# A decode attention kernel on one core: the last 64 rows of wq land as half rows on all 128 partitions, and the filler products of the tail are regrouped

## The chip, the core and the metric

The kernel runs on one core of one Trainium2 chip. The core has five engines that run side by side and meet at semaphores: TensorE (PE, matrix products and weight loads), VectorE (DVE), ScalarE (ACT), GpSimd (POOL) and SyncE (SP, which here only issues transfers). Sixteen DMA engines carry the transfers. The metric is the device time of one execution in microseconds; a change is judged by the median of several runs against runs of the kernel before on the same chip.

## The reference

Two independent problems, A and B, are computed and their outputs laid side by side. Each is one decode step (one query per sequence) of attention over a cache window with two query heads per cache head:

```
B, Sq, D = 2, 1, 576;  Hq, Hkv, Sk, Dh = 32, 16, 16384, 128
W = min(4096, max(256, Sk // 4))                      # 4096: the last 4096 cache rows
q = (x @ wq).reshape(B, Sq, Hq, Dh).transpose(0, 2, 1, 3)
k = repeat(k_cache[:, :, Sk - W:, :], 2, axis=1)      # v the same
p = softmax(einsum("bhqd,bhkd->bhqk", q, k) * Dh ** -0.5)
o = einsum("bhqk,bhkd->bhqd", p, v)
out = o.transpose(0, 2, 1, 3).reshape(B, Sq, Hq * Dh) @ wo
```

All tensors are bfloat16. wq is 576 x 4096 and wo is 4096 x 576 in each problem. The cache windows are what is large: 1 MB for each problem, batch and cache head, 128 MB in all for K and V.

## The kernel before

**Slabs and the ring.** Everything large goes through `ring`, four buffers of 128 partitions x 32 KB (4 MB each). The list `stream` (lines 198 to 206) gives the order: the first 512 rows of wq for A, the same for B, then K and V slabs alternating (K0, K1, V0, K2, V1, ...), each slab holding four (batch, head) pairs of 4096 cache rows. SP issues all of these transfers in that order (`issue_slab`, `issue_wq`, `issue_wo`); before it issues slab n it waits until the reader of slab n-4 is done, because that is the buffer it overwrites. The pieces of wo (`wob`) are issued at fixed places of the stream. The last V slab is cut in two pieces (`PIECES`: three quarters and one quarter of it). The wo rows of the last group come as one transfer for the heads of the group's first slab and three for those of its second slab: heads (0,1), head 2 and head 3 (`HEADS`, `issue_last`), each with its own semaphore.

**The front.** D is 576 = 4 x 128 + 64, so wq is four chunks of 128 rows (the ring slab) and 64 remaining rows. `issue_wq` lands these remaining rows in the tile `wqr`, which has 128 partitions: A's rows on the even partitions and B's on the odd ones, 8 KB a row. x of the two problems sits in `x_sb` on four partitions (two per problem). For the chunk of remaining rows, line 361 copies each of the 64 values to two neighbouring columns, multiplied by a mask (`maskP`) that keeps only the column of the own problem (`x_dup`); then `f_xT` (line 346) transposes the five chunks on PE, and `f_xev` (line 367, ACT) spreads them into the stationary operand `xT`, which has `NXC` = 5 chunks per problem. `do_qpair` (line 396) makes q for two groups of heads at a time: five chunks times four banks, 20 products of 128 x 512, in two operations of which the first ends with the last product of the first group. Even pairs write the score banks `st`, odd pairs the banks `tb0`, `tb1`, `ot` and `acc`; `do_qrow` (ACT, then DVE, then ACT) takes q out of a group's banks. The third pair uses the banks of the first again and waits for them, and so on (`prev`).

**The middle.** For each K slab, DVE transposes it in four pieces (line 485), PE makes the scores (line 510 and its repeats through the helper at line 170), DVE finds the maxima, ACT takes the exponentials, DVE transposes the result, and PE multiplies it with the V slab (line 601). Every two slabs the heads of a group are normalised, spread (`do_redist`) and multiplied with wo (`do_proj`). The order of all this is written out by hand in lines 804 to 893; each engine works its list in order, and an instruction waits on semaphores for what it depends on.

**The tail.** After the last K slab come, on PE: the product with the first piece of the last V slab; `do_redist` of the last group (line 882), with two filler products of 128 x 512 on data that nobody reads (`f_idle`, line 711); the product with the second piece; two more filler products with a weight load of their own (`keep_on`, line 727, called at line 884); the collection of the last slab's heads (line 648); the product of the last group's first four heads with wo (line 760, which also waits for the last of `fin_ops`, DVE's copy at line 783 of the sums so far into the bank of the outputs); and the products of the last four heads, of which heads (0,1), head 2 and head 3 each wait for their own piece of wo. Then ACT and DVE take half of B's outputs each (lines 792 and 793), and two transfers write them.

Of the kernel before, what the change touches and what calls it, by code (L numbers as in the profile page):

```python
# [59 lines left out]
def build_kernel(nc, probs, out, cfg=None):  # L60
    cfg = dict(cfg or {})
    NR = cfg.get("NR", 4)
# [6 lines left out]
    NPROB = len(probs)  # L69
    Bb, _one, D = x0.shape  # L70
    _, Hkv, Sk, Dh = k0.shape
    HD = wq0.shape[1]
# [14 lines left out]
    DREM = D - 128 * NFC  # L87
    assert DREM * 2 == 128 and NFC * HD == SLABW
    HH = HD // 2
    NXC = NFC + 1  # L90
    NOUT = wo0.shape[1]
    NH = NOUT // 2
    NB0 = 512
# [13 lines left out]
    with es:  # L107
        sb = lambda name, shape, dt: es.enter_context(nc.sbuf_tensor(name, shape, dt))
        ring = sb("ring", [128, NR, SLABW], BF16)
        xt = sb("xt", [128, NKT, 2048], FP32)  # L110
        wqr = sb("wqr", [128, HD], BF16)
        wob = sb("wob", [128, 2, 8, NOUT], BF16)
        xT = sb("xT", [128, NXC, NPROB, 128], BF16)
        x_dup = sb("x_dup", [NPROB * Bb, DREM, NPROB], BF16)
        maskP = sb("maskP", [NPROB * Bb, NPROB], BF16)
# [44 lines left out]
        ring_sem = [sem("ring%d" % r) for r in range(NR)]  # L160
        wq_sem = sem("wq")
        wo_sem = [sem("wo%d" % r) for r in range(2)]
        x_sem = [sem("xload%d" % P) for P in range(NPROB)]
        wl_sem = [sem("wl%d" % n_) for n_ in range(len(HEADS))]
        out_sem = sem("outdone")
        piece_sem = [sem("piece%d" % n_) for n_ in range(NPC)]
# [15 lines left out]
            return op  # L182

        def load_x(P, eng):
            return dma_op(eng, x_sem[P], 1, lambda e: e.dma_start(
                x_sb[P * Bb:(P + 1) * Bb, :], probs[P][0][:, 0, :]).then_inc(x_sem[P], 16), [], "xload%d" % P)
# [57 lines left out]
        def issue_wq(n, P):  # L244
            wqP = probs[P][3]
            r = n % NR
            deps = [reader[n - NR]] if n >= NR else []
            wq_dma[P] = dma_op("sp", wq_sem, 1, lambda e: e.dma_start(
                wqr[P::NPROB, :], wqP[NFC * 128:D, :]).then_inc(wq_sem, 16), [], "wqr%d" % P)
            slab_dma[n] = dma_op("sp", ring_sem[r], 1, lambda e: e.dma_start(  # L250
                ring[:, r, :], wqP[0:NFC * 128, :].rearrange("(p s) n -> p (s n)", s=NFC)).then_inc(ring_sem[r], 16), deps, "wq%d" % P)

            if P == 0:
                for P_ in range(1, NPROB):
                    x_dma[P_] = load_x(P_, "sp")
# [89 lines left out]

        def f_xT(e, bank):
            last = None
            bb = bank[:].bitcast(BF16)
            NB = NPROB * Bb
            for ch in range(NXC):  # L350
                if ch < NFC:
                    src = x_sb[0:NB, 0:NFC * 128].rearrange("b (p s) -> b s p", s=NFC)[:, ch, :]
                else:
                    src = x_dup[0:NB, :, :].rearrange("b r t -> b (r t)")
                last = e.transpose(bb[:, ch * NB:(ch + 1) * NB], src, ident_b[0:NB, 0:NB])  # L355
            return last
        issue_until(0)
        init_small()
        init["maskP"] = S.add("dve", lambda e: e.tensor_reduce(
            maskP[:], ident_b[0:NPROB * Bb, 0:NPROB * Bb].rearrange("d (p b) -> d p b", b=Bb), AX.X, ALU.max), [p_ident_b], "maskP")  # L360
        x_cd = S.add("dve", lambda e: e.tensor_tensor(  # L361
            x_dup[:], x_sb[:, NFC * 128:D].unsqueeze(2).broadcast_to([NPROB * Bb, DREM, NPROB]),
            maskP[:].unsqueeze(1).broadcast_to([NPROB * Bb, DREM, NPROB]), ALU.mult), [init["maskP"]] + list(x_dma.values()), "xdup")

        n_x, bank_x, op_xT = tb_job(f_xT, "xT", list(x_dma.values()) + [x_cd, p_ident_b])

        def f_xev(e):
            NB = NPROB * NXC
            return e.activation(
                xT[:].rearrange("c h p (a w) -> c (h p) a w", a=4)[:, :, :, 0:Bb],  # L370
                bank_x[:].bitcast(BF16)[:, 0:NB * Bb].rearrange("c (p b) -> c p b", b=Bb).unsqueeze(2).broadcast_to([128, NB, 4, Bb]),
                ACTF.Copy)
        op_xev = S.add("act", f_xev, [op_xT, p_zxT], "xev")
        tb_consumer[n_x] = op_xev

        def init_mask():
# [318 lines left out]
        def do_redist(G, idle=0):  # L695
# [14 lines left out]
            if idle:  # L710
                def f_idle(e):
# [11 lines left out]
            tb_consumer[n] = r_ev[G]  # L723

        fin_ops = []

        def keep_on(n):
            def f(e):
                first = last = e.matmul(idle_out, ident_b[:, :], maskB[:, :], start=True, stop=True)
# [264 lines left out]
```

## Time and profile before

| what | value |
|---|---|
| median of three runs | 363.33 us (363.29 to 363.35) |
| the profiled execution's own time | 363.62 us |
| its span, first to last instruction | 362.3 us |
| DMA: moved, mean rate | 153.27 MB, 423 GB/s |
| busy share of the span | PE 62%, DVE 56%, ACT 19%, POOL 10% |
| first wqr transfer: issue at, landing after | 0.80 us, 3.7 us |
| second wqr transfer: issue at, landing after | 2.41 us, 13.2 us |
| first q product | at 15.70 us |
| last PE product | 360.25 us and 0.31 us long |

The span is what the profile covers; the own time of the profiled execution is 1.3 us longer, for what lies around the program. Busy shares are averages over the whole span and matmul ends are modelled. A row of a group list gives the line, the engine, the operation, output and input tile, the number of instructions, the busy time and the mean of one, and the idle time before them with what ended it. A row of a timeline gives start, length, and what. Names such as `st` stand for both buffers `st0` and `st1`.

### The profile page before, as it was taken

How to read it: one execution, taken by the hardware profiler on the slowest of the kernel's cores; microseconds unless marked ns; L12 is line 12 of the kernel's file. 1: busy time of each engine (PE TensorE's matmuls, PEld its weight loads, DVE VectorE, ACT ScalarE, POOL GpSimd, SP SyncE). 2: the span in 40 equal slices, each digit the busy share in tenths (PEclk: the TensorE clock that was granted, in tenths of full speed). 3: DMA queues.
4: the chain of work that ended last, by engine and by line, in shares of the span. 5: the costliest groups of instructions: out<-in, count | busy, mean ns of one | idle time of the engine just before them, and what ended most of it. 6: DMA issues, size and time to landing. Idle time of an engine off the chain costs nothing.

```text
span 362.3 us, 2755 instructions
## 1 busy us (share of the span) xinstructions
PE 224.9 (62%) x1325; PEld 57.4 (16%) x950; DVE 201.5 (56%) x175; ACT 68.7 (19%) x153; POOL 35.3 (10%) x55
## 2 busy tenths in 40 slices
PE   0399195474865647584774747575673738656775
PEld 0000021111221201111121112111121112211121
DVE  3013598483917467291936648092854839179831
ACT  1036402020300303020210203112020203002131
POOL 1000000004000040004000040001200040110020
PEclk9999589788796968889787889969697887969999
DMA  8999999999999999999999999999999999999996
GB/s 348 405 445 423 445 408 433 456 412 442 420 426 434 434 409 447 430 438 430 402 454 430 434 434 418 434 434 430 421 434 430 438 425 430 430 434 434 425 419 242
DMA packets 6943, 153.27 MB, mean 423 GB/s; under 512 B 778, under 2 KB 1300, under 8 KB 1428
## 3 DMA queue, kind: packets, MB, share of 16 engines
q1 hardware_dynamic: 6924, 153.10, 98.7%
q8 instruction: 9, 0.15, 0.2%
q14 instruction: 2, 0.02, 0.0%
q10 hardware_dynamic: 8, 0.00, 0.0%
HBM read 153.10 MB, written 0.00 MB: 423 GB/s over the span
## 4 chain that ended last, share of the span: by engine, by line
DMA 71%; DVE 14%; PE 13%; SPq 1%; issue 0%
DMA ring<-in_B_k_cache_dram 34%; DMA ring<-in_A_k_cache_dram 26%; DVE xt L485 13%; DMA wob<-in_B_wo_dram 8%; PE st L170 6%; DMA wqr<-in_B_wq_dram 4%; PE st L510 4%; PE st L421 1%; PE tb L170 1%; PE acc L170 1%; PE ot L170 1%; DVE nM L533 1%; PE tb L421 0%; PE tb L523 0%; SPq L237 0%
## 5 line engine op out<-in xcount | busy, mean ns | idle before, releaser
L485 DVE STREAM_TRANSPOSE xt<-ring 128x2048 f32<-128x2048 f32 x64 | 145.3, 2285 | 77.3 <-DMA ring<-in_B_k_cache_dram 40.1
L510 PE MATMUL st<-xt,zq 128*128 128x512 bf16 x256 | 115.8, 452 | 114.5 <-DVE xt L485 88.8
L170 PE MATMUL st<-xt,zq 128*128 128x512 bf16 x256 | 114.4, 447 | 0.0
L510 PEld LDWEIGHTS st<-xt,zq 128*128 128x128 bf16 x256 | 27.9, 109 | 210.0 <-DVE xt L485 104.1
L601 PE MATMUL acc<-ring,pC 128*32 128x512 bf16 x512 | 33.9, 381 | 2.6 <-DMA ring<-in_B_v_cache_dram 2.6
L538 ACT ACTIVATE nMrep<-nM 1x128 f32<-1x128 f32 x16 | 4.9, 308 | 142.9 <-DVE nM L533 142.9
L613 ACT ACTIVATE acc_sb<-acc 128x512 bf16<-128x512 f32 x16 | 9.5, 597 | 81.3 <-PE acc L601 81.3
L563 DVE STREAM_TRANSPOSE pC<-pR 128x1024 bf16<-128x1024 bf16 x16 | 19.5, 1216 | 3.6 <-ACT pR L555 2.1
L520 DVE TENSOR_REDUCE m<-st 128x1 f32<-128x1024 f32 x16 | 19.0, 1190 | 1.2 <-PE st L170 1.2
L620 POOL TENSOR_TENSOR acc_sb<-acc_sb,maskJ 128x1024 bf16<-128x1024 bf16 (+1 forms) x8 | 13.4, 1679 | 59.0 <-ACT acc_sb L613 59.0
L472 POOL TENSOR_TENSOR zq<-qk,maskA 128x128 bf16<-128x128 bf16 x16 | 6.3, 399 | 127.9 <-PE st L170 106.1
L555 ACT ACTIVATE pR<-st,bias_sb 128x1024 bf16<-128x1024 f32 x16 | 17.8, 1114 | 0.5
L445 DVE STREAM_TRANSPOSE qtr<-qrow 128x512 f32<-128x512 f32 x8 | 5.7, 712 | 20.8 <-ACT qrow L435 13.5
L387 ACT ACTIVATE st<-maskB 128x1024 f32<-128x1024 bf16 x16 | 16.5, 1032 | 1.6 <-POOL rsel L570 0.4
L756 PE MATMUL ot<-wob,Rsb 128*2 128x512 bf16 x56 | 15.7, 399 | 0.2 <-ACT Rsb L721 0.2
L601 PEld LDWEIGHTS acc<-ring,pC 128*32 128x32 bf16 x512 | 12.9, 95 | 16.1 <-DMA ring<-in_B_v_cache_dram 3.6
L570 POOL TENSOR_TENSOR rsel<-maskS,rsum 128x16 f32<-128x16 bf16 x8 | 1.7, 216 | 124.1 <-ACT pR L555 124.1
L170 PE MATMUL tb<-wob,Rsb 128*2 128x64 bf16 x56 | 11.1, 197 | 0.0
L355 PE MATMUL tb<-ident_b,x_sb 4*128 4x4 bf16 x4 | 0.3, 173 | 14.6 <-DVE x_dup L361 14.6
L775 DVE TENSOR_TENSOR o_rest<-o_rest,tb 2x64 f32<-2x64 f32 x3 | 0.6, 209 | 15.4 <-PE tb L170 15.4
L623 POOL TENSOR_TENSOR acc_sb<-acc_sb 128x512 bf16<-128x512 bf16 (+1 forms) x8 | 8.2, 1030 | 0.6
L533 DVE TENSOR_REDUCE nM<-tb 1x8 f32<-1x128 f32 x16 | 4.4, 272 | 6.2 <-PE tb L523 6.1
(88 smaller groups left out, 107.0 us busy)
## 6 DMA issues: line engine op xcount, KB each, us to landing
ring<-in_A_k_cache_dram SPq DMA_DIRECT2D x8, 4096.0 KB, 30.8
ring<-in_A_v_cache_dram SPq DMA_DIRECT2D x8, 4096.0 KB, 32.1
ring<-in_B_k_cache_dram SPq DMA_DIRECT2D x8, 4096.0 KB, 30.7
ring<-in_B_v_cache_dram SPq DMA_DIRECT2D x7, 4096.0 KB, 32.8
wob<-in_A_wo_dram SPq DMA_DIRECT2D x4, 1152.0 KB, 33.5
ring<-in_A_wq_dram SPq DMA_DIRECT2D x1, 4096.0 KB, 12.8
ring<-in_B_wq_dram SPq DMA_DIRECT2D x1, 4096.0 KB, 22.4
wob<-in_B_wo_dram SPq DMA_DIRECT2D x3, 1152.0 KB, 34.6
```

What stands on the lines that cost most here:

```text
L170: return e.add_instruction(mybir.InstMatmult(name=nc.get_next_instruction_name(), engine=i.engine, ins=[e.lower_ap(rhs), i.ins[1]], outs=[ ...
L387: chain[(s, "fill")] = S.add("act", lambda e: e.activation(ST[s % 2][:, :].rearrange("k (h j) -> k h j", h=2), maskB[:].unsqueeze(1).broad ...
L485: Xop[(s, u)] = S.add("dve", lambda e: e.transpose(xt[:, i % NKT, :].rearrange("k (j w) -> k j w", w=64), ring[:, n % NR, :].bitcast(FP32) ...
L510: first = last = e.matmul(bank, zq[:, p4, s % NZQ, w0:w0 + 128], mv, start=False, stop=stop, skip_group_check=True)
L520: chain[(s, "max")] = S.add("dve", lambda e: e.tensor_reduce(m1[:, 0:1], ST[s % 2][:, :], AX.X, ALU.max), d, "max%d" % s)
L555: chain[(s, "exp")] = S.add("act", lambda e: e.activation(pR[:, :], ST[s % 2][:, :], ACTF.Exp, bias=bias_sb[:, 0:1], scale=SCALE, accum_ou ...
L563: chain[(s, "pC")] = S.add("dve", lambda e: e.transpose(pC[:, s % NPT, :, :].rearrange("k j c -> k (j c)"), pR[:, :]), d, "pC%d" % s)
L601: last = e.matmul(ACC[32 * cb:32 * cb + 32, 0:512], pC[:, D_ % NPT, j0_:j0_ + 4, :].rearrange("k j c -> k (j c)"), ring[:, n % NR, j0_ * 1 ...
L613: acc_ev[D_] = S.add("act", lambda e: e.activation(acc_sb[:, D_ % 2, :], ACC[:, :], ACTF.Copy), d, "accev%d" % D_)
L620: t = S.add("pool", lambda e: e.tensor_tensor(v, v, maskJ[:].unsqueeze(1).unsqueeze(3).broadcast_to([128, l1 - l0, 4, 128]), ALU.mult), [a ...
L623: t = S.add("pool", lambda e: e.tensor_tensor(a_[:, :, 0:256], a_[:, :, 0:256], a_[:, :, 256:512], ALU.add), [t], "acca%d" % D_)
L756: first = e.matmul(OT[0:Bb, 0:NB0], l_, wob[:, pc, s_, 0:NB0], start=start and begin, stop=end, skip_group_check=True)
```

## The change

- `wqr` becomes 128 partitions x 2 problems x 4 KB. Each of the 64 remaining rows is landed as two half rows (columns 0 to 2047 and 2048 to 4095) on two neighbouring partitions, for each problem in a slot of its own. The bytes are the same; a transfer now writes 128 rows of 4 KB and no longer 64 rows of 8 KB.
- `NXC` becomes 6. The chunk of remaining rows stands twice in `xT`: once kept on the even partitions alone and once on the odd ones. `x_dup` is a plain doubled copy, `maskP` is now 128 partitions x 2, made behind it on DVE; the ACT evacuation does the first four chunks, and a new DVE operation (`xev2`) writes the two masked ones. `f_xT` uses products with a spread identity in place of transposes.
- In `do_qpair`, the two banks of the lower column half use the even chunk and the other two the odd one: still 20 products a pair, with one weight load more. The second operation of a pair waits, in addition, until the banks of the previous pair have been taken out (`before`).
- The two x transfers share one semaphore.
- In the tail, `do_redist` is called with three filler products in place of two, these wait for `fin_ops` too, and `keep_on` (two filler products and a weight load) is removed. The separate wait of the last heads for their pieces of wo is as before.

```diff
-    NXC = NFC + 1
+    NXC = NFC + 2
...
-        wqr = sb("wqr", [128, HD], BF16)
+        wqr = sb("wqr", [128, NPROB, HH], BF16)
...
-        x_sem = [sem("xload%d" % P) for P in range(NPROB)]
+        x_sem = sem("xload")
...
             wq_dma[P] = dma_op("sp", wq_sem, 1, lambda e: e.dma_start(
-                wqr[P::NPROB, :], wqP[NFC * 128:D, :]).then_inc(wq_sem, 16), [], "wqr%d" % P)
+                wqr[:, P, :], wqP[NFC * 128:D, :].rearrange("r (h n) -> r h n", h=2)).then_inc(wq_sem, 16), [], "wqr%d" % P)
...
-                last = e.transpose(bb[:, ch * NB:(ch + 1) * NB], src, ident_b[0:NB, 0:NB])
+                last = e.matmul(bank[:, ch * 4 * NB:(ch + 1) * 4 * NB], src, ident_b[0:NB, 0:NB].rearrange(
+                    "k (p b) -> k p b", b=Bb).unsqueeze(2).broadcast_to([NB, NPROB, 4, Bb]), start=True, stop=True)
...
+        x_cd = S.add("dve", lambda e: e.tensor_copy(
+            x_dup[:], x_sb[:, NFC * 128:D].unsqueeze(2).broadcast_to([NPROB * Bb, DREM, 2])), list(x_dma.values()), "xdup")
         init["maskP"] = S.add("dve", lambda e: e.tensor_reduce(
-            maskP[:], ident_b[0:NPROB * Bb, 0:NPROB * Bb].rearrange("d (p b) -> d p b", b=Bb), AX.X, ALU.max), [p_ident_b], "maskP")
-        x_cd = S.add("dve", lambda e: e.tensor_tensor(
-            x_dup[:], x_sb[:, NFC * 128:D].unsqueeze(2).broadcast_to([NPROB * Bb, DREM, NPROB]),
-            maskP[:].unsqueeze(1).broadcast_to([NPROB * Bb, DREM, NPROB]), ALU.mult), [init["maskP"]] + list(x_dma.values()), "xdup")
+            maskP[:], ident_b[:].rearrange("d (r t) -> d t r", t=2), AX.X, ALU.max), [p_ident_b], "maskP")
...
         op_xev = S.add("act", f_xev, [op_xT, p_zxT], "xev")
+        NB_ = NPROB * 4 * Bb
+
+        def f_xev2(e):
+            return e.tensor_tensor(
+                xT[:, NFC:NXC].rearrange("c h p (a w) -> c h (p a) w", a=4)[:, :, :, 0:Bb],
+                bank_x[:, NFC * NB_:(NFC + 1) * NB_].rearrange("c (q b) -> c q b", b=Bb).unsqueeze(1).broadcast_to([128, 2, NPROB * 4, Bb]),
+                maskP[:].unsqueeze(2).unsqueeze(3).broadcast_to([128, 2, NPROB * 4, Bb]), ALU.mult)
+        op_xev = S.add("dve", f_xev2, [op_xev, op_xT, init["maskP"]], "xev2")
...
-            order = [NFC] + list(range(NFC))
+            mine = lambda ch: [b for b in range(4) if ch < NFC or b % 2 == ch - NFC]
+            order = [NFC, NFC + 1] + list(range(NFC))
...
-            todo_ = [(ch, b) for ch in order for b in range(4)]
+            todo_ = [(ch, b) for ch in order for b in mine(ch)]
...
-                        w_ = ring[:, nq % NR, ch * HD + c0:ch * HD + c0 + 512] if ch < NFC else wqr[:, c0:c0 + 512]
+                        w_ = ring[:, nq % NR, ch * HD + c0:ch * HD + c0 + 512] if ch < NFC else wqr[:, P, c0 - (b % 2) * HH:c0 - (b % 2) * HH + 512]
...
-                op = S.add("pe", fn, [slab_dma[nq], op_xev] + list(wq_dma.values()) + prev, "q%d" % Gs[g])
+                before = [q_free.get((i - 1, b)) for b in range(4)] if g else []
+                op = S.add("pe", fn, [slab_dma[nq], op_xev] + list(wq_dma.values()) + prev + before, "q%d" % Gs[g])
...
-                S.add("pe", f_idle, [chain[(ND - 1, "exp")], init["maskB"]], "idle%d" % G)
+                S.add("pe", f_idle, [chain[(ND - 1, "exp")], init["maskB"]] + fin_ops, "idle%d" % G)
...
-        def keep_on(n):
-            def f(e):
-                first = last = e.matmul(idle_out, ident_b[:, :], maskB[:, :], start=True, stop=True)
-                for _ in range(n - 1):
-                    last = matmul_again(e, first, idle_out, maskB[:, :], True, True)
-                return last
-            S.add("pe", f, [chain[(ND - 1, "exp")], init["maskB"]], "keep%d" % n)
...
-        do_redist(D_ // 2, 2)
+        do_redist(D_ // 2, 3)
         do_PV(D_, range(PIECES[1][0] // JR, PIECES[1][1] // JR), pieces[1])
-        keep_on(2)
         do_comb(D_)
```

More of the change, by code (lines that the diff above doesn't have):

```diff
@@ L110, in build_kernel @@
         xt = sb("xt", [128, NKT, 2048], FP32)
-        wqr = sb("wqr", [128, HD], BF16)
+        wqr = sb("wqr", [128, NPROB, HH], BF16)
         wob = sb("wob", [128, 2, 8, NOUT], BF16)
         xT = sb("xT", [128, NXC, NPROB, 128], BF16)
-        x_dup = sb("x_dup", [NPROB * Bb, DREM, NPROB], BF16)
-        maskP = sb("maskP", [NPROB * Bb, NPROB], BF16)
+        maskP = sb("maskP", [128, 2], BF16)
+        x_dup = sb("x_dup", [NPROB * Bb, DREM, 2], BF16)
         x_sb = sb("x_sb", [NPROB * Bb, D], BF16)
@@ L184, in load_x @@
         def load_x(P, eng):
-            return dma_op(eng, x_sem[P], 1, lambda e: e.dma_start(
-                x_sb[P * Bb:(P + 1) * Bb, :], probs[P][0][:, 0, :]).then_inc(x_sem[P], 16), [], "xload%d" % P)
+            return dma_op(eng, x_sem, 1, lambda e: e.dma_start(
+                x_sb[P * Bb:(P + 1) * Bb, :], probs[P][0][:, 0, :]).then_inc(x_sem, 16), [], "xload%d" % P)
         x_dma = {0: load_x(0, "act")}
@@ L347, in f_xT @@
             last = None
-            bb = bank[:].bitcast(BF16)
             NB = NPROB * Bb
-            for ch in range(NXC):
+            for ch in range(NFC + 1):
                 if ch < NFC:
@@ L358, in build_kernel @@
         init_small()
+        x_cd = S.add("dve", lambda e: e.tensor_copy(
+            x_dup[:], x_sb[:, NFC * 128:D].unsqueeze(2).broadcast_to([NPROB * Bb, DREM, 2])), list(x_dma.values()), "xdup")
         init["maskP"] = S.add("dve", lambda e: e.tensor_reduce(
-            maskP[:], ident_b[0:NPROB * Bb, 0:NPROB * Bb].rearrange("d (p b) -> d p b", b=Bb), AX.X, ALU.max), [p_ident_b], "maskP")
-        x_cd = S.add("dve", lambda e: e.tensor_tensor(
-            x_dup[:], x_sb[:, NFC * 128:D].unsqueeze(2).broadcast_to([NPROB * Bb, DREM, NPROB]),
-            maskP[:].unsqueeze(1).broadcast_to([NPROB * Bb, DREM, NPROB]), ALU.mult), [init["maskP"]] + list(x_dma.values()), "xdup")
+            maskP[:], ident_b[:].rearrange("d (r t) -> d t r", t=2), AX.X, ALU.max), [p_ident_b], "maskP")
         n_x, bank_x, op_xT = tb_job(f_xT, "xT", list(x_dma.values()) + [x_cd, p_ident_b])
         def f_xev(e):
-            NB = NPROB * NXC
+            NB = NPROB * NFC * 4
             return e.activation(
-                xT[:].rearrange("c h p (a w) -> c (h p) a w", a=4)[:, :, :, 0:Bb],
-                bank_x[:].bitcast(BF16)[:, 0:NB * Bb].rearrange("c (p b) -> c p b", b=Bb).unsqueeze(2).broadcast_to([128, NB, 4, Bb]),
+                xT[:, 0:NFC].rearrange("c h p (a w) -> c (h p a) w", a=4)[:, :, 0:Bb],
+                bank_x[:, 0:NB * Bb].rearrange("c (q b) -> c q b", b=Bb),
                 ACTF.Copy)
         op_xev = S.add("act", f_xev, [op_xT, p_zxT], "xev")
+        NB_ = NPROB * 4 * Bb
[5 more added lines that the diff above has]
+        op_xev = S.add("dve", f_xev2, [op_xev, op_xT, init["maskP"]], "xev2")
         tb_consumer[n_x] = op_xev
```

## The prediction

> **What bounds the kernel now.** I read the rates of the page first, then the queues, the chain of waits, and the timeline of the first and last microseconds. On the page:
>
> ```profile
> span 362.3 us, 2755 instructions
> ...
> DMA  8999999999999999999999999999999999999996
> GB/s 348 405 445 423 445 408 433 456 412 442 420 426 434 434 409 447 430 438 430 402 454 430 434 434 418 434 434 430 421 434 430 438 425 430 430 434 434 425 419 242
> DMA packets 6943, 153.27 MB, mean 423 GB/s; under 512 B 778, under 2 KB 1300, under 8 KB 1428
> ...
> q1 hardware_dynamic: 6924, 153.10, 98.7%
> q8 instruction: 9, 0.15, 0.2%
> ```
>
> The reader is to see that the transfers on SP's queue alone keep the sixteen DMA engines busy for 98.7% of the span, 357.6 of 362.3 us. What is left over is 2.15 us before the first packet and 2.5 us behind the last (359.83), both from the trace's packet records. No other engine is busy beyond 62%. The kernel is one gapless stream of transfers; compute can change the time only by starting the stream later, by letting it run dry, or behind its end. The end, in the chain of waits:
>
> ```profile
> 332.25 27.95 DMA wob<-in_B_wo_dram
> 360.20 0.04 issue
> 360.25 0.31 PE st L760 x2
> 360.56 0.02 issue
> 360.58 0.45 DVE out_sb L793
> ```
>
> The last two products stand 0.05 us behind the landing of head 3's piece of wo, issued 28 us earlier. PE's timeline shows what fills the time ahead of it:
>
> ```profile
> 356.57 0.38 PE L170 MATMUL st<-maskB,om 128*128 128x512 bf16 x1
> ...
> 357.37 0.61 PE L601 MATMUL acc<-ring,pC 128*32 128x512 bf16 x8 [0.42 <-DMA ring<-in_B_v_cache_dram]
> ...
> 357.92 0.39 PE L729 MATMUL st<-maskB,ident_b 128*128 128x512 bf16 x1
> 358.04 0.60 ACT L613 ACTIVATE acc_sb<-acc 128x512 bf16<-128x512 f32 x1 [1.33 <-PE acc L601]
> 358.14 0.38 PE L170 MATMUL st<-maskB,ident_b 128*128 128x512 bf16 x1
> ...
> 358.69 0.26 PE L648 MATMUL tb<-ident_r,acc_sb 128*128 128x8 bf16 x4 [0.17 <-ACT acc_sb L613]
> ```
>
> **The change, part by part.** The sum is made against the profiled execution's own 363.62 us; the median of the runs is 0.29 us lower, and the result is carried over to it.
>
> *The half rows.* Two transfers of 64 packets of 8 KB become two of 128 packets of 4 KB: four packets more for each DMA engine and transfer. The trace's packet records give medians of 312 ns for 8,192 bytes and 181 ns for 4,608; on the line through both, 4,096 bytes take 162 ns. Two half rows are thus 324 ns, 12 more than a row, and 2 transfers x 4 rows an engine x 12 ns is **+0.10 us** on the stream, with nothing to hide it. Bounds: while the last V piece and wo move in rows of 8 and 4.6 KB (354 to 358 us) the stream runs at 395 GB/s with a DMA share of 0.99, against 422 at 1.00 for 342 to 346. At 399 and 422 GB/s, 1.05 MB take 2.63 and 2.49 us: +0.14 above. Below: all 8,192-byte packets together took 0.42 us an engine more than at their quickest (309 ns), mostly in the first transfer; if writing all partitions removed that, -0.4. I take +0.10, since these rows differ from it in size alone.
> The Trainium skill, page "DMA: Bandwidth & Descriptors", section "Why small descriptors are slow", speaks against the change too: a fixed three cycles or so beside one cycle for 32 bytes, per packet. By that rule two half rows would be 262 cycles against 259, some 0.03 us in all as an estimate; the row's 12 ns is the larger.
>
> *The first issue.* The 64-row transfer took SP 0.56 us (the second 0.48); those of 128 rows take 0.57 and 0.61 (line 250) and 0.60 (line 275). Only the first delays the stream: between -0.08 and +0.05, taken as +0.02.
>
> *x, masks and evacuation.* B's x is what this waits for (DVE starts line 361 at 14.22). The plain copy costs what the masked one did, 0.28. `maskP`, now 128 wide like line 331's to 343's reductions (0.23 to 0.37), runs beside PE's five products. ACT's evacuation ends near 15.15; behind it comes `xev2`, between 0.16 (line 665) and 0.42 (line 687, larger), taken as 0.2, so x is ready near 15.45 while B's wqr lands at 15.56. Even 0.4 us late it would only move the q products. `maskC` and `maskB` are pushed back as much; their first reader is ACT's fill at 33.35. The wider memset of xT (0.59 x 768/640 = 0.71) ends long before 14.22.
>
> *The q products.* 20 a pair as before; one weight load more a pair is 0.10, and loads overlap products (0.4 for four if none did). In odd pairs the first operation ends one product later, 0.22, while ACT is still at the previous group. The added waits stand before the last products of a pair. Second pair: ACT has emptied the first pair's banks by 25.36, the product comes at 26.45: no wait. Third: 29.91 against about 30.5: none. Fourth: ACT ends at 35.35, the product stood at 35.08, so PE waits some 0.3 us, and behind it SP's issue of K2 (35.49), which needs that product. With all slips K2 is issued under 1 us later. It landed 32.83 us after issue, of which 4 MB at 430 GB/s are 9.8: 23 us of other bytes stood before it. So **0**; without that cover it would be up to 1 us. Later slabs are issued 25 to 30 us ahead as well.
>
> *The tail.* The third filler product ends near 356.57 + 3 x 0.22 = 357.23; the second V piece's product starts at 357.37 behind its landing: 0.14 us to spare. The added wait is for DVE's copy at line 783, done at 353.84, 2.7 us earlier; PE's whole tail is queued behind it. Removing `keep_on` (357.91 to 358.52) leaves PE idle until 358.69, when ACT is done; nothing moves up. One semaphore wait of PE falls away ahead of line 760, and head 3's landing at 360.20 covers that. So 0; if cover failed, -0.05 to +0.2.
>
> The sum is +0.10 + 0.02 = **+0.12**: 363.74 for such a profiled execution, and 363.33 + 0.12 = **363.45** for the median.
>
> **The rivals.** About 0.2%, 0.73 us, is what a measurement of this kernel tells from no change.
>
> 1. *An instruction fetch falls badly: slower.* The nine packets of the instruction queue are 16 KB each and come every 249 to 272 PE instructions; each of the first eight holds one DMA engine for 0.96 to 1.10 us, by the packet records. At 359.0 us nine engines still had packets and the others had ended by 358.7, so the engines that gave way to a fetch seem to end the stream. The ninth, at 359.73, found the stream 0.1 us from its end. Should it start before an engine's last packet of head 3's wo and hit one that already had a fetch, the end comes up to **+1.0** us later: 364.4. The changed program counts 1,318 products, 945 weight loads and 5 waits and drains on PE, the old one 1,319, 942 and 7: 2,268 both, and the last 40 instructions are the same but for a wait, so I expect every fetch where it was.
> 2. *PE's clock falls in the tail: slower.* Granted clock changes come 3.41 us apart. Stretches of that length with PE busy for 1.33 to 1.43 us lost the full clock (64.82, 139.92 and 180.88), those with 1.49 to 1.55 kept it (78.48, 307.17, 351.54). The one from 354.95 to 358.37 has 2.92 and would have 2.7. Were it lost at 358.37, lines 648 on would run at half speed: line 760's two sets of eight products, 0.66 us each without waits, twice as long, end at 358.88 + 2.64 = 361.52 against 360.56, **+0.96**: 364.4. After the change no stretch of 3.41 us that begins between 355 and 358 has less than 1.8 us of PE.
> The Trainium skill, "TensorE: Matmul & The Clock Gate", Part 1, has these windows free-running, not tied to the kernel's start, so that the drop could fall elsewhere in another execution. One trace can't show that; three runs within 0.06 us speak against its mattering here.
> 3. *The spread pays: faster.* Writing 128 partitions takes away the slow packets of the first transfer: -0.4 + 0.02, 362.95, still within 0.2%. To pass 0.73 us it would have to take 30% off the 2.5 us that the two transfers last.
> 4. *The half rows are not what is moved*, and transfers stay as they were: 363.33. The listing shows 128 x 2048 for both, so hardly.
>
> **How the numbers follow.** The stream as it is with 0.12 us more (with 4): 0.80, its own range 363.1 to 363.9 from the bounds above. Fetch: 0.07. Clock: 0.05. Spread: 0.08, of which 0.04 beyond 0.2%. Faster 0.04, same 0.83, slower 0.13 (the two slower cases and 0.01 of the first). For 8 in 10 the range goes from 363.0, near rival 3, to 364.0, short of rivals 1 and 2.
>
> **What would show it.** In the changed profile: 128 packets more (7,071) and 256 more under 8 KB (1,684); the DMA line at 9 from the second slice to the last but one; the chain of waits again ending in wo's landing, PE, DVE; PE's first q product between 15.5 and 16.0; no row at `keep_on`, and idle before line 657 (648 before) of some 0.7 us. The prediction is wrong if DMA stops being busy in the middle, if the last landing comes more than 0.5 us later relative to the first packet, or if the granted clock drops before 360 us.

## The result, and the profile after

The changed kernel takes 364.65 us (median of 22 runs, 364.25 to 365.26); the kernel before took 363.65 us on the same chip. The ratio is 1.0026, with an interval of 1.002 to 1.0033: slower by a quarter of a per cent, outside the forecast range. The profiled execution took 364.93 us, 1.31 more than that of before.

The page of the changed kernel:

```profile
span 363.7 us, 2756 instructions
...
DMA  8999999999999999999999999999999999999994
GB/s 346 418 447 404 461 390 430 461 404 459 415 413 451 414 451 420 447 418 447 414 424 447 418 442 429 425 440 420 414 451 436 429 431 433 422 440 422 425 417 185
DMA packets 7071, 153.27 MB, mean 421 GB/s; under 512 B 778, under 2 KB 1300, under 8 KB 1684
...
q1 hardware_dynamic: 7052, 153.10, 98.4%
q8 instruction: 9, 0.15, 0.2%
```

The packets are the ones forecast (7,071, of which 1,684 under 8 KB), and the stream has no hole: the DMA line stands at 9 up to the last slice but one. The last slice is what changed: 4 tenths and 185 GB/s, where it was 6 tenths and 242. Fewer engines work there, for longer. The end of the chain of waits:

```profile
331.12 29.50 DMA wob<-in_B_wo_dram
360.61 0.14 issue
360.75 1.14 PE st L761 x8
361.89 0.02 issue
361.91 0.45 DVE out_sb L794
```

A landing of wo still ends the kernel, but the chain now runs through the piece of heads (0,1), landed at 360.61, and eight products follow it, not two. PE's and ACT's timeline shows from where on things are late:

```profile
357.31 0.61 PE L610 MATMUL acc<-ring,pC 128*32 128x512 bf16 x8 [0.24 <-DMA ring<-in_B_v_cache_dram]
357.97 0.60 ACT L622 ACTIVATE acc_sb<-acc 128x512 bf16<-128x512 f32 x1 [1.36 <-PE acc L610]
...
358.63 0.26 PE L657 MATMUL tb<-ident_r,acc_sb 128*128 128x8 bf16 x4 [0.70 <-ACT acc_sb L622]
...
358.81 0.66 PE L761 MATMUL st<-wob,Rsb 128*2 128x288 bf16 x8
...
360.75 1.12 PE L761 MATMUL st<-wob,oTn 128*2 128x288 bf16 x8 [1.28 <-DMA wob<-in_B_wo_dram]
```

The last two of these PE rows in the kernel before, whose rows ahead of them stand in the prediction:

```profile
358.88 0.66 PE L760 MATMUL st<-wob,Rsb 128*2 128x288 bf16 x8
359.60 0.94 PE L760 MATMUL st<-wob,oTn 128*2 128x288 bf16 x8
```

Up to 358.81 each row is some 0.06 us earlier than in the kernel before. Then PE stands 1.28 us for wo. So most of the loss lies between the landing of the second V piece and that of the last rows of wo, on the DMA side: the last packet of wo ends 1.10 us later. The rest, some 0.2 us, lies behind it: the granted clock fell to a half at 360.57, while PE stood waiting, and the last eight products took 0.40 to 0.45 us each where they had taken 0.28.

The trace's packet records say what else ran there. They list nine packets of 16,384 bytes on the instruction queue (q8 on the page). Each lasts about 1 us; through the first eight of them, which lie inside the stream, 15 data packets are under way, as an average, and not 16. So each holds one DMA engine:

```
                     first data  instruction packet no. 9  last packet of wo
before               2.15 us     359.73 us, 1.26 us long   ends 359.83 us
after                1.83 us     358.36 us, 1.08 us long   ends 360.93 us
```

The ninth packet came 1.37 us earlier, into the stream instead of at its end, and the last packet of wo ended 1.10 us later. That is the mechanism of the first rival, and its price. The runs below ask whether that is the cause, and what moved the packet.

### The profile page after: what moved, and what is told of

Read it like the earlier page. It is cut to its first block, busy times and chain, and to the rows that moved or that the text cites. A ratio compares the mean times of both kernels' runs of the same rounds, so it can differ in the third digit from the quotient of the medians.

```text
span 363.7 us, 2756 instructions
## 1 busy us (share of the span) xinstructions
PE 227.5 (63%) x1324; PEld 58.1 (16%) x953; DVE 201.8 (55%) x176; ACT 68.7 (19%) x153; POOL 35.3 (10%) x55
## 2 busy tenths in 40 slices
DMA packets 7071, 153.27 MB, mean 421 GB/s; under 512 B 778, under 2 KB 1300, under 8 KB 1684
## 4 chain that ended last, share of the span: by engine, by line
DMA 72%; DVE 15%; PE 9%; ACT 3%; SPq 1%; issue 0%
DMA ring<-in_B_k_cache_dram 34%; DMA ring<-in_A_k_cache_dram 26%; DVE xt L494 13%; DMA wob<-in_B_wo_dram 8%; PE st L170 4%; PE st L519 4%; DMA wqr<-in_B_wq_dram 4%; ACT qrow L444 1%; DVE qtr L454 1%; ACT qk L462 1%; PE st L429 1%; DVE nM L542 1%; ACT qrow L449 1%; PE tb L532 0%; PE st L761 0%
## 5 line engine op out<-in xcount | busy, mean ns | idle before, releaser
L757 PE MATMUL ot<-wob,Rsb 128*2 128x512 bf16 x56 | 16.9, 421 | 0.2 <-ACT Rsb L730 0.2
L776 DVE TENSOR_TENSOR o_rest<-o_rest,tb 2x64 f32<-2x64 f32 x3 | 0.6, 210 | 15.5 <-PE tb L170 15.5
```

Source lines behind the costliest of these rows:

```text
L757: first = e.matmul(OT[0:Bb, 0:NB0], l_, wob[:, pc, s_, 0:NB0], start=start and begin, stop=end, skip_group_check=True)
```

## The experiments

All compare with runs of the kernel before on the same chip (363.45 to 363.54 us). "Place" is the number, in PE's program, of the first weight load of the second V piece's products (line 601 before, 610 after), counting weight loads, products, separate semaphore waits and one drain from zero. It is the quantity that the study ended with, so it stands in the table from the start; the earlier expectations argue from other quantities. The row-sum products in float32 count once there, though the trace has two loads and two products for each. e7, which turns them into bfloat16, is 2,211 by the count of its program; the table gives it the 16 records that it saves as 16 places less.

| run | edit | place | ninth packet at, us | wo ends, us | median us | ratio to before |
|---|---|---|---|---|---|---|
| before | - | 2,207 | 359.73 | 359.83 | - | 1 |
| after | the change | 2,211 | 358.36 | 360.93 | 364.65 | 1.0026 (1.002 to 1.0033) |
| e1 | after, separate wait back in the tail | 2,211 | 358.58 | 361.14 | 364.92 | 1.0035 (1.0022 to 1.0048) |
| e2 | before, that wait moved to the fillers | 2,207 | 359.53 | 359.77 | 363.51 | 1.0001 (0.9992 to 1.001) |
| e3 | front of after, tail of before | 2,210 | 358.57 | 361.19 | 364.60 | 1.0029 (1.0018 to 1.0041) |
| e4 | before, 20 small products in the front | 2,227 | 358.63 | 361.24 | 364.68 | 1.0035 (1.0023 to 1.0048) |
| e5 | after, two fillers | 2,210 | 358.76 | 361.43 | 364.92 | 1.0036 (1.0022 to 1.0049) |
| e6 | before, one small product | 2,208 | none recorded | 359.80 | 363.55 | 1.0004 (0.9993 to 1.0014) |
| e7 | after, row sums in bf16 | 2,195 | 359.22 | 359.38 | 363.22 | 0.9988 (0.9978 to 0.9999) |
| e8 | before, 237 small products | 2,444 | 344.38 | 361.06 | 364.79 | 1.0033 (1.0021 to 1.0046) |
| e9 | after, one filler | 2,209 | 359.33 | 359.60 | 363.36 | 0.9995 (0.9986 to 1.0003) |
| e10 | before, two small products | 2,209 | 362.20 | 359.80 | 363.60 | 1.0005 (0.9996 to 1.0015) |
| e11 | e6 and e2 together | 2,208 | 359.59 | 359.59 | 363.50 | 0.9998 (0.999 to 1.0007) |
| e12 | e1 and e5 together | 2,210 | 357.97 | 360.78 | 364.69 | 1.0029 (1.0018 to 1.0041) |
| e13 | before, three small products | 2,210 | 358.54 | 361.10 | 364.89 | 1.0038 (1.0023 to 1.0053) |
| e14 | e13 without `keep_on` | 2,210 | 358.55 | 361.22 | 365.01 | 1.0041 (1.0026 to 1.0056) |
| e15 | e9 with `keep_on` | 2,209 | 359.11 | 359.28 | 363.17 | 0.9989 (0.9979 to 0.9999) |
| e16 | e9 with one small product | 2,210 | 358.10 | 360.66 | 364.66 | 1.0035 (1.0022 to 1.0048) |

Two readings of the table need no theory. First, the time goes with the ninth packet without exception: where it starts at 358.76 or earlier, wo ends at 360.66 or later and the kernel takes 364.6 to 365.0; where it starts at 359.11 or later, or isn't recorded, wo ends by 359.83 and the kernel takes 363.2 to 363.6. Nothing lies between these medians. It holds for single executions too, by the spans on record: 361.7 to 362.8 us in the second group, 363.0 to 364.2 in the first. (In 17 of 105 executions of before, e6 and e10 the time is 1.6 to 3.1 us longer than the span, where in all others it is 1.2 to 1.4. The ninth packets of these three come last of all, or aren't recorded; no run asks why.) Second, the half rows stand in both groups (after, e1, e3, e5, e12, e16 against e7, e9, e15).

A third reading shows how a packet costs what it does. Each large transfer has sixteen landing records in the trace, read here as one for each DMA engine. These are the landings of the last piece of wo, head 3's:

```
before   8 from 358.28 to 359.10   8 from 359.86 to 360.20
after    8 from 358.20 to 359.29   7 from 359.82 to 360.08   1 at 361.35
e8       8 from 358.10 to 359.23   7 from 359.82 to 360.11   1 at 361.47
```

In the kernel before, the landings that stand apart behind the others are as many as the instruction packets so far, in each transfer from the first such packet on: one, then two, up to eight. An engine that has given way to a packet thus stays behind for the rest of the stream, and the first eight packets fell on eight different engines. All ten kernels with the ninth packet in the stream have one landing 1.3 to 1.5 us behind the other fifteen there, which leaves seven in the group before it: the ninth packet came back to an engine that already had one. In the eight other kernels the last landing is 0.03 to 0.26 us behind the fifteenth.

### First batch: is it the moved wait, the front, or the place?

e1 puts one line of the change back, e2 does that line alone, e3 takes the front of the changed kernel with the tail of the old one, and e4 leaves the old kernel as it is, but for 20 idle one-column products ahead of the q products.

```diff
 e1, from after (e2 is the reverse, from before)
-                S.add("pe", f_idle, [chain[(ND - 1, "exp")], init["maskB"]] + fin_ops, "idle%d" % G)
+                S.add("pe", f_idle, [chain[(ND - 1, "exp")], init["maskB"]], "idle%d" % G)
 e3, from after: the line of e1, and
-        do_redist(D_ // 2, 3)
+        do_redist(D_ // 2, 2)
...
+        keep_on(2)
 e4, from before
+        def f_count(e):
+            first = last = e.matmul(TB[1][:, 0:1], ident_b[:, :], ident_b[:, 0:1], start=True, stop=True)
+            for _ in range(18):
+                last = matmul_again(e, first, TB[1][:, 0:1], ident_b[:, 0:1], True, True)
+            return last
+        S.add("pe", f_count, [p_ident_b], "count")
```

> The changed kernel with one part undone: the filler products no longer wait for the copies of the sums, so that wait stands again by itself ahead of the products of the last group's first four heads. Everything else is as changed (half rows, three filler products, the later two gone). Theory F (fetch): the separate wait holds PE's instruction reading back until the last slab's heads are collected (about 358.7 us); without it the ninth instruction fetch came 1.4 us earlier (358.36 in place of 359.73 us) and held an engine that still had wo rows for 1.08 us. So the ninth fetch goes back to about 359.6 us, the last wo landing to 360.2 or earlier, and the time to 363.1 to 363.6 us, 1 us or more under the changed kernel. Theory R (rows): the half rows delay one DMA engine, the time stays at 364.4 to 364.8. Theory C (clock or the missing filler products): also 364.4 to 364.8.

> The kernel before with this one edit: the filler products wait for the copies of the sums too, so the separate wait ahead of the first four heads' products is gone. No half rows, and all four filler products stay. Theory F: the ninth fetch comes before 358.7 us and the time is 364.2 to 364.8, about 1 us over the kernel before. Theories R and C: as the kernel before, within 0.2 us.

> The changed front alone (half rows, doubled and masked x chunk, products in the new order, the added waits between pairs) with the tail of the kernel before. Theory F: the ninth fetch at about 359.6, no slower than before; the first packet starts 0.33 us earlier as in the changed kernel's trace (1.83 against 2.15 us), so 363.0 to 363.4. Theory R: 364.4 to 364.8. Theory C: as theory F.

> The kernel before with 20 more PE instructions (one weight load, 19 products of one column) ahead of the first transposes, in time in which PE waits for x anyway. Tail, waits and transfers are untouched; only the place of the 256-instruction blocks in the program moves, by 20 instructions towards earlier work. Theory F, if the block boundary sets off the fetch: the ninth fetch is set off ahead of the separate wait, comes before 358.7 us and the time is about 1 us longer, 364.2 to 364.8, with no other change. If only the wait itself matters and not the boundary: no change, within 0.2 us. Theories R and C: no change.

The theory that the removed wait alone lets PE read ahead fell in both directions: with the wait back nothing is won (364.92), with the wait gone from the old kernel nothing is lost (363.51). e3, which that theory put at 363.0 to 363.4, took 364.60 and shows that the tail isn't needed for the loss. e4 is the run that carries the case: its transfers, waits and tail are those of the kernel before, it only has 20 instructions more far ahead, and it loses the same 1.2 us, with the packet at 358.63. So the loss needs no half rows. How many instructions stand ahead is enough.

### Second batch: where is the threshold?

```diff
 e5, from after
-        do_redist(D_ // 2, 3)
+        do_redist(D_ // 2, 2)
 e6, from before, in do_qpair
+                    if i == 0 and part[-1] == todo_[-1]:
+                        last = matmul_again(e, q_first[1], TB[1][:, 0:1], ident_b[:, 0:1], True, True)
 e7, from after
-        rsel = sb("rsel", [128, 2, 8], FP32)
+        rsel = sb("rsel", [128, 2, 8], BF16)
...
-            n, bank, op = tb_job(lambda e, bank: e.matmul(bank[:, 0:16], ones_f[:, :], rsel[:].rearrange("k l c -> k (l c)"),
+            n, bank, op = tb_job(lambda e, bank: e.matmul(bank[:, 0:16], ones_b[:, :], rsel[:].rearrange("k l c -> k (l c)"),
 e8, from before: f_count of e4 with range(235)
```

e7 changes a part of the computation: the row sums of the softmax are rounded to bfloat16 before they are added over the partitions. PE then runs each of these eight products in one pass, and the trace has 16 PE records fewer, all ahead of the V piece.

> The changed kernel with two filler products in place of three: one PE instruction less ahead of the collection of the last slab's heads; the moved wait stays, the later two filler products stay away, half rows stay. Theory B (place of the block): the four slow kernels so far have 2,227 or more PE instructions ahead of that collection's first weight load, the two fast ones 2,226; a 256-instruction block begins between, and PE's reading stops at that load until about 358.6 us. With one less (2,226) the ninth fetch comes after the load is released, at about 359.5 to 359.7, and the time falls by some 1.2 us to 363.1 to 363.5. Theory W (the moved wait) and theory R (half rows): stays at 364.4 to 364.9.

> The kernel before with one PE product more (one column, behind the first pair's q products, some 330 us ahead of the tail): 2,227 PE instructions ahead of the collection of the last heads. Nothing else differs. Theory B: the ninth fetch comes at 358.4 to 358.6 and the time rises to 364.4 to 364.9. Theories W and R: no change, 363.3 to 363.7.

> The changed kernel with the eight products that add up the row sums in bfloat16 in place of float32 (the row sums are rounded to bfloat16 ahead of them). The float32 ones are two products and two loads each in the trace, so 16 PE instructions less ahead of the tail. Theory B: the block begins 15 instructions behind the released load, among the products with wo, so the ninth fetch comes at 359.7 to 360.3, at or behind the end of the stream, and the time is 363.0 to 363.4. The alternative, that the fetch's place does not matter: 364.4 to 364.9.

> The kernel before with 237 more PE instructions (one weight load and 236 products of one column) in PE's idle time ahead of the first transposes. A block still begins 20 instructions behind the released load, so the fetch in the tail should be at or behind the end of the stream (now the tenth), but nine fetches in place of eight fall into the stream. If the ninth hits a DMA engine that had none so far: the time stays at 363.3 to 363.7. If it comes back to an engine that already had one: about 1 us more, 364.2 to 364.8. A delay of the first products by up to 1 us is covered by the transfers queued.

e5 and e6 missed: the threshold was not where the place of the waiting load (line 648/657) had put it. e7 came as expected: with 16 fewer PE records ahead, everything else of the change in place, the packet falls behind the stream again and the kernel takes 363.22 us. e8 came as its second case said. It moves the ninth packet far forward, to 344.38, and the end is as late as with one at 358.5: the V piece's product starts at 358.69 instead of 357.37, because one of the sixteen landings of that piece comes 1.39 us behind the others. (Its stream also began 0.39 us later than that of the kernel before, at 2.54.) So the price doesn't hang on the packet meeting the last rows of wo; 14 us ahead of them it costs the same.

### Third batch: a rule that fitted everything so far, and missed

A rule with two places fitted the ten kernels: PE reads nine instructions past the load that waits for the copies of the sums, but not past a separate wait. Four runs were chosen so that it had to decide.

```diff
 e9, from after
-        do_redist(D_ // 2, 3)
+        do_redist(D_ // 2, 1)
 e10, from e6: the added product twice
+                        last = matmul_again(e, q_first[1], TB[1][:, 0:1], ident_b[:, 0:1], True, True)
 e11: e6 with the line of e2.  e12: e1 with the line of e5.
```

> The changed kernel with one 128-column filler product in the tail where it had three; half rows, masks and the moved wait as in the change. Theory P (PE reads its program nine loads and products past a waiting weight load, not past a separate wait, and the ninth 16,384-byte instruction packet is set off early, near 357.4 us, if that reading reaches the 2,232nd load or product): the load that waits for the copies of the sums is the 2,222nd, the reading stops at 2,231, and the ninth packet lies at 359.2 or later, the last packet of wo at about 359.4 to 359.8, the time 363.0 to 363.5, ratio to before at most 1.000. Rival (the front or the half rows cost the 1.2 us, whatever the tail holds): packet at 358.4 to 358.8, last packet of wo near 361.0, time 364.4 to 364.9.

> The kernel before with two one-column products more in the q products, where one more left its time at 363.55. Theory P: the separate wait ahead of the last products comes after 2,232 loads and products (with one more: 2,231), the reading reaches the edge, the ninth packet lies at 358.4 to 358.8, the last packet of wo at 360.9 to 361.3, the time 364.4 to 364.9, ratio 1.0025 to 1.004. Rival (it is the number of instructions up to some larger amount, or the half rows): as with one more, 363.4 to 363.7, no ninth packet before 359.2.

> The kernel before with one one-column product more in the q products and the wait for the last heads' sums moved onto the idle products, so that no separate wait stands there; each of the two alone left the time as before (363.55 and 363.51). Theory P: without the separate wait the reading goes nine past the waiting load, 2,223 + 9 = 2,232, the ninth packet lies at 358.4 to 358.8, the last packet of wo at 360.9 to 361.3, the time 364.4 to 364.9. Rival (each is harmless, and so both together are): 363.4 to 363.7.

> The changed kernel with two fillers where it had three and with the separate wait back ahead of the last products; each of the two alone left the time at 364.92. Theory P: the separate wait comes after 2,231 loads and products, the reading stops there, the ninth packet lies at 359.2 or later, the last packet of wo at 359.4 to 359.8, the time 363.0 to 363.5. Rival (each alone changed nothing, so both together don't): 364.5 to 365.1, packet at 358.4 to 358.8.

Only e9 came as this rule said; e10, e11 and e12 went the other way (363.60, 363.50, 364.69). The rule was fitted after the fact to ten results, with two free numbers; it is dropped. What the fourteen kernels do share is one place further ahead: that of the second V piece's products, 2,209 and less on one side, 2,210 and more on the other.

### Fourth batch: that place, with either front

e13 and e14 reach 2,210 with the front of before. e15 keeps 2,209 with the half rows while all that stands behind the V piece moves three places back. e16 goes from e9's 2,209 to 2,210 by a product in the front.

```diff
 e13, from e6: the added product three times.   e14, from e13
-        keep_on(2)
 e15, from e9: keep_on is defined again, and
+        keep_on(2)
         do_comb(D_)
 e16, from e9: the added product of e6
```

> The kernel before with three one-column products more in the q products (with one and two more it took 363.55 and 363.6). Theory Q (the ninth packet is set off early when the first weight load of the second V piece's products is the 2,210th of PE's program or a later one; here 2,210, with two more 2,209): packet at 358.0 to 358.8, last packet of wo at 360.9 to 361.3, time 364.4 to 364.9. Rival H (the half rows or their front are needed, and the small amounts don't count): 363.4 to 363.7.

> The kernel before with three one-column products more in the q products and without the two products that keep PE on behind the second V piece; the load of the V piece is again the 2,210th, all that is behind it stands three places earlier. Theory Q: packet at 358.0 to 358.8, time 364.4 to 364.9. Rival K (what counts is the place of the load that waits for the copies of the sums, here 2,226 as in the kernel before): packet at 359.2 or later, 363.4 to 363.7.

> The changed kernel with one filler in place of three and with the two products that keep PE on put back behind the second V piece. The V piece's load is the 2,209th, the waiting load the 2,228th. Theory Q: packet at 359.2 or later, time 363.1 to 363.6. Rival K (the waiting load's place counts; with the half rows 2,226 was enough to be early): packet at 358.0 to 358.8, 364.4 to 364.9.

> The changed kernel with one filler, and one one-column product more in the q products: the V piece's load is the 2,210th, the waiting load the 2,226th, as with two fillers (364.92), but PE has one 0.4 us product less in the tail. Theory Q: packet at 358.0 to 358.8, time 364.4 to 364.9. Rival (it is the time that the fillers take and not their number): as with one filler, 363.36.

All four came as theory Q said. e10 and e13 differ by one product of one column, 340 us ahead of the end, and by 1.29 us of time (they ran on different chips; the kernel before took 363.50 and 363.54 there). The ends of their timelines, first e10 (two small products):

```profile
358.71 0.26 PE L651 MATMUL tb<-ident_r,acc_sb 128*128 128x8 bf16 x4 [0.17 <-ACT acc_sb L616]
...
358.90 0.66 PE L763 MATMUL st<-wob,Rsb 128*2 128x288 bf16 x8
...
359.60 0.93 PE L763 MATMUL st<-wob,oTn 128*2 128x288 bf16 x8
```

and e13 (three):

```profile
358.72 0.26 PE L652 MATMUL tb<-ident_r,acc_sb 128*128 128x8 bf16 x4 [0.17 <-ACT acc_sb L617]
...
358.91 0.66 PE L764 MATMUL st<-wob,Rsb 128*2 128x288 bf16 x8
...
360.92 0.29 PE L764 MATMUL st<-wob,oTn 128*2 128x288 bf16 x2 [1.35 <-DMA wob<-in_B_wo_dram]
```

PE does the same things within 0.01 us up to 358.91. Then one of them has its rows of wo, and the other waits 1.35 us.

e15 is the best version that needs no other rounding: 363.17 us, 0.9989 of the kernel before (0.9979 to 0.9999), half rows and all. Its page and the end of its chain of waits:

```profile
span 361.8 us, 2757 instructions
...
DMA  8999999999999999999999999999999999999996
...
q1 hardware_dynamic: 7052, 153.10, 98.8%
```

```profile
331.84 27.82 DMA wob<-in_B_wo_dram
359.67 0.04 issue
359.71 0.31 PE st L769 x2
360.02 0.02 issue
360.04 0.45 DVE out_sb L802
```

The last slice is at 6 tenths again, and head 3's two products stand behind the last landing, as in the kernel before, 0.5 us earlier. Its interval ends just short of 1, and the difference is about half of the 0.2% that the forecast called measurable.

## Why the prediction was wrong

**The bound was read rightly.** Transfers set the end in every run; only the last packet of wo moved the time. The rows of PE and ACT in the tail came as forecast: the third filler hidden, the moved wait satisfied, PE idle 0.70 us ahead of line 657.

**The half rows** were forecast at 12 ns a row from a line through two packet sizes. The records give a median of 159 ns for 4,096 bytes (forecast 162) and 313 for a row of 8,192 left whole, so two half rows cost 5 ns more than a row, and not 12: +0.04 us in place of +0.10. On the stream, from its first packet to its last, the three kernels with half rows and a late ninth packet take 357.77 (e9), 357.54 (e7) and 357.45 us (e15), the kernel before 357.68: +0.09 to -0.23 us. The bounds of -0.4 to +0.14 hold; but the kernels with whole rows and no ninth packet in the stream spread just as far (357.32 in e11 to 357.68), so these single traces show no cost or gain of the half rows.

**The first issue** was mis-sized: forecast +0.02 with bounds of -0.08 to +0.05, measured -0.32 on the first packet. SP's rows, of the kernel before and then of the changed one:

```profile
0.80 0.56 SPq L248 DMA_DIRECT2D wqr<-in_A_wq_dram  x1
1.42 0.57 SPq L250 DMA_DIRECT2D ring<-in_A_wq_dram  x1
```

```profile
0.80 0.40 SPq L248 DMA_DIRECT2D wqr<-in_A_wq_dram  x1
1.26 0.42 SPq L250 DMA_DIRECT2D ring<-in_A_wq_dram  x1
```

0.56 became 0.40, which is half of the 0.32; the other half lies between the end of that issue and the first packet (0.79 us before, 0.63 after). But the second row, an issue that the change doesn't touch, fell too, from 0.57 to 0.42. That the rows of other 128-row issues carry over was therefore the wrong reading. Why they all got shorter isn't settled; in e13, with the front of before, the two are 0.56 and 0.57 again. In e15 the last packet of wo ends 0.55 us earlier than in the kernel before (359.28 against 359.83); its first packet is 0.32 earlier.

**x, masks, evacuation, q products:** costed at nothing, and rightly. The first q product starts at 15.39 us (15.70 before; forecast 15.5 to 16.0, without the earlier start); `xev2` took 0.19 us (forecast 0.2).

**PE's clock** (second rival) held as long as it was forecast to, and then fell to a half at 360.57 us, just ahead of the last eight products, which had waited for wo. From 357.16 to 360.57 PE was busy for 1.46 us; the forecast's "less than 1.8" for no such stretch counted on these products 1.2 us earlier. From wo's last packet to the end of PE it takes 0.94 us in place of 0.70. The same happened in e1, e5 and e16 (0.94 to 0.95), while e3, e4, e8, e12, e13 and e14 kept the clock (0.73 to 0.75) and are as slow. So the clock is a small part that follows from the wait, not the cause.

**The step that failed** stands in the first rival: "2,268 both, and the last 40 instructions are the same but for a wait, so I expect every fetch where it was". The total is no measure of where a fetch falls. The change adds four weight loads in the q products and a filler, and takes a separate wait away from the front: the V piece's products move from place 2,207 to 2,211. `keep_on` goes too, which brings the total back to 2,268, but it stands behind the V piece, where it doesn't count (e14, e15). The threshold of this program is at 2,210, three places from where the old kernel stood. The mechanism and the price (up to +1.0, 364.4; the medians differ by 1.00) were in the text. That the price agrees so well is partly luck: the engine with two packets falls 1.3 to 1.5 us behind the others, not 1.0, the halved clock adds some 0.2 in the profiled execution, and the median of the kernel before is 363.65 here where it was 363.33 in the forecast. The chance of 0.07 was far too low for a stream that a fetch can lengthen and a place that was never counted.

The Trainium skill, page "Runtime: NRT & Kernel Launch", section "Instruction fetch mechanics", has instructions come in blocks of 16 KiB, 256 instructions each, and the cost of a boundary "mostly hidden". The size agrees: from the second packet to the eighth PE does 1,534 instructions in the changed kernel and 1,560 in the kernel before, 256 and 260 a packet. "Hidden" doesn't hold here: PE doesn't wait for the instructions, but the packet takes some 1.1 us of one DMA engine from a stream that sets the end.

**What stays open.** Shown is that the ninth packet's time decides the 1.2 us, that it does so by putting one engine behind all others, and that the place of the V piece's products decides the packet's time. The prediction had read the first half of this: "the engines that gave way to a fetch seem to end the stream". Why the ninth packet comes back to an engine that had one, when eight engines had none, isn't known; it did so in all ten kernels. Nor is it shown how PE's reading comes to depend on this place and not on what stands behind it: the rule of place 2,210 was found from fourteen kernels, and four runs chosen to test it kept to it. That e6 records no ninth packet, and e10 one at 362.20, behind the stream, fits the late side, but no run says why they are later than the 359.1 to 359.7 of the others.

## What to carry to other kernels

Where transfers set the end, the instruction stream is one of the transfers: count how many 16 KB instruction packets fall ahead of the last data packet, and how close the next one is to joining them. Count the places up to what PE does while the last data move, not the total; here one product of one column, 340 us ahead of the end, cost 1.2 us. The packets ahead of it cost too: in this kernel every one of them puts its engine behind for good, and the end is set by the engine with the most. When a version comes out 0.3% off, add or take away one idle product before the edit itself is judged: with one filler and `keep_on` kept, the same half rows gain a little where they seemed to lose.

## What the hardware showed that was not expected

- A step in time of 1.29 us from one idle product of one column (e10 to e13), with every other PE row within 0.01 us.
- Each packet of the instruction queue left one of the sixteen landings of every later transfer behind the others, by 0.7 to 1.4 us in the kernel before; two on one engine left it 1.3 to 1.5 us behind all the rest.
- Packets of the instruction queue took 0.90 to 1.26 us for 16,384 bytes, while 8,192 bytes of data took 0.31 us, and with a ninth one in the stream wo ended 0.8 to 1.6 us later than the 359.83 of the kernel before, wherever it fell, at 344.38 as at 358.55.
- SP's four issues of wq got shorter by a quarter when two of them changed form (0.56, 0.57, 0.48, 0.61 to 0.40, 0.42, 0.34, 0.47 us), and the first packet came 0.32 us earlier. The first three repeat within 0.01 us in the other traces with half rows; the fourth varies there from 0.43 to 0.61.
